# Attention and token-mixing MLP in one kernel: a ramp by halves of 256 tokens, a halved last pass, quarter-row MLP pieces, and a planner without its table of rules

## The chip, the cores and the metric

The kernel runs on one core of one Trainium2 chip. The metric is the device time of one launch in microseconds (us). Before the change it is 755.73 us, the median of 3 runs (755.54 to 755.74).

## What is computed

For 2048 tokens of width 640, with 32 heads of width 20:

```python
xn = layernorm(x)
q, k, v = xn @ wqkv                        # 32 heads of 20
s = softmax(q @ k.T * 20 ** -0.5) @ v @ wo # s: [2048, 640]
u = gelu(w1.T @ layernorm(xn) + b1)        # over tokens: 2048 -> 1536
y = w2.T @ u + b2                          # 1536 -> 2048
out = x + s * silu(y)
```

The attention has 32 heads x 2048 queries x 2048 keys of scores, and each score needs an exponential. The MLP mixes along the tokens, not along the features.

## The kernel before, in words

**Units and passes.** Heads go in 8 groups G of four. A pass is one group and 512 queries, so there are 32 passes (`passes`, L852). In a pass the keys come in 16 chunks of 128. A unit is one head, one chunk and 512 queries: a score tile of 128 keys x 512 queries that fills one PSUM bank. A pass has 64 units and the program 2048. A head's 20 rows are padded to 32, so the four heads of a group lie in the four row groups of the PE array. One visit of PE to the scores (`emit_st`, L1206) runs up to four units side by side, one in each row group.

**Two ways to take an exponential.** ACT takes most units: one Exp over two or three banks (`emit_exp`, L1235) from PSUM to the ring `pt_sb` (20 slots). DVE takes the others. It turns a score into a bf16 bit pattern by an add and a maximum (`emit_op1`, L1246), and for each four units of a chunk it makes three shifted copies (`emit_top`, L1268). The weighted sum of four such patterns stands for the exponential. Only the chunks in `RC` may go to DVE. The weighted sums with v (`emit_pv`, L1284) add up in the bank `AB`; at the end of a pass `ep_steps` (L1400 to L1421) transposes that bank, divides by the row sums and stores.

**Banks.** Two ACT groups of three banks (0 to 2, 3 to 5), the bank `AB` of the sums, and one bank `JB` for everything else. The third bank of an ACT group can be lent to a DVE unit (`LEND`), and then the Exp covers two banks.

**The rest of the work** is cut in jobs that take bank `JB` one after the other: projections for the next groups (`dqk_steps`), v (`v_steps`), the two MLP matmuls (`mlp_steps`, 16 or 12 steps of K=128 for 512 columns, each step four 32-column matmuls side by side at L644) with their activations (`act_steps`, L829 to L845), and the output projection (`op_mms`, L929) with its product (L944) and the residual (L954).

**Order of work.** All of it is fixed on the host. A planner keeps a reckoned clock for each engine, with a cost for each instruction (`mm`, `dv`, `ac`) and a hand-over time between engines (`Prog.lat`). At each turn it takes, on the engine that is free first, the candidate of the best priority (`pe_cands`, `eng_cands`). A switch of PE between scores, sums and full matmuls counts some 105 ns (`pe_cost`). `act_deadline` says by when the next scores are due, and `SLACK` by how much other work may overrun that. `PLAN` is a table of rules: for each 16 units it picks one of the values in `OPTS` for 14 settings (`tune`).

**Ramp.** x comes in six DMAs of one to four 128-token blocks. `ln_steps` takes the statistics of a block on DVE (L531, L533, L538, L542), the inverse root on POOL (L545) and applies it on DVE (L549). The first 512 tokens are transposed on PE (L598), the others by DMA (L586). `qk_steps` (L629) makes q and k of group 0, `v_steps` (L737) v. `wp_step` (L720) copies the first 80 columns of wq and wk into padded form on ACT. The ramp ends for the planner when the last v (`v0_14`) and the last q (`qk0_0_3`) are made; only then do DVE units begin.

**Tail.** The last pass ends with its transposes by halves (L1392 to L1396). The last 512 tokens are then finished: matmuls for what is known already (L929) before, the last head group's part (L934) after, products with the gate (L1607, L1623), the residual (L1609, L1625) and four stores (L1616).

The softmax here doesn't subtract the row's maximum and nothing guards it: scores larger than these inputs give would overflow.

## Time and profile before

| what | value |
|---|---|
| median of 3 runs | 755.73 us |
| span of the profiled execution, first to last instruction | 753.7 us |
| left between the span and the median | 2.0 us (755.73 - 753.7) |
| ACT busy | 729.9 us (97%), 695 instructions |
| DVE busy | 721.0 us (96%), 1320 instructions |
| PE busy | 717.6 us (95%), 10302 matmuls |
| POOL busy | 15.6 us (2%) |
| DMA | 42.54 MB, mean 56 GB/s |

The page gives no time of its own for the profiled execution besides its span. So the 2.0 us between the span and the median are what lies around it, and I take them as fixed. "Busy" is the time in which an engine has at least one instruction running. For PE it also holds waiting in its pipeline, so three figures near 96% don't say which engine sets the end. The chain of waits and a table by stages tell that.

### The profile page before, as it was taken

How to read it: one execution, taken by the hardware profiler on the slowest of the kernel's cores; microseconds unless marked ns; L12 is line 12 of the kernel's file. 1: busy time of each engine (PE TensorE's matmuls, PEld its weight loads, DVE VectorE, ACT ScalarE, POOL GpSimd, SP SyncE). 2: the span in 40 equal slices, each digit the busy share in tenths (PEclk: the TensorE clock that was granted, in tenths of full speed). 3: DMA queues.
4: the chain of work that ended last, by engine and by line, in shares of the span. 5: the costliest groups of instructions: out<-in, count | busy, mean ns of one | idle time of the engine just before them, and what ended most of it. 6: DMA issues, size and time to landing. Idle time of an engine off the chain costs nothing.

```text
span 753.7 us, 23158 instructions
## 1 busy us (share of the span) xinstructions
PE 717.6 (95%) x10302; PEld 240.7 (32%) x10302; DVE 721.0 (96%) x1320; ACT 729.9 (97%) x695; POOL 15.6 (2%) x22
## 2 busy tenths in 40 slices
PE   9999999999999999999999999999999988998997
PEld 7432223222323232323223323233333232222222
DVE  8869999999999999999999999999999999999997
ACT  4999999999999999999999999999999999999993
POOL 4200000000000000000000000000000000000001
PEclk9999999999999999999999999999999999999999
DMA  9584111110313031121014022223124340011011
GB/s 245 109 167 57 38 26 38 20 36 7 86 14 77 13 68 38 35 61 21 7 37 111 26 49 52 47 54 102 44 57 82 76 150 11 6 47 48 13 47 36
DMA packets 117143, 42.54 MB, mean 56 GB/s; under 512 B 75300, under 2 KB 115876, under 8 KB 116996
## 3 DMA queue, kind: packets, MB, share of 16 engines
q1 hardware_dynamic: 117044, 41.07, 23.9%
q8 instruction: 80, 1.31, 0.7%
q14 instruction: 19, 0.16, 0.1%
HBM read 26.37 MB, written 10.22 MB: 49 GB/s over the span
## 4 chain that ended last, share of the span: by engine, by line
ACT 85%; PE 12%; DVE 2%; DMA 1%; issue 0%; POOL 0%
ACT pt_sb L1235 83%; PE ps_all L1284 4%; PE ps_all L644 4%; PE ps_all L1206 4%; ACT zt_sb L840 1%; ACT zt_sb L835 1%; PE ps_all L929 1%; DMA xnT_sb<-regC 1%; DVE bst_sb L531 0%; DVE bst_sb L533 0%; DMA regA<-in_A_x_dram 0%; DVE regC L549 0%; DVE regC L1607 0%; PE ps_all L683 0%; DVE xnT_sb L611 0%
## 5 line engine op out<-in xcount | busy, mean ns | idle before, releaser
L1235 ACT ACTIVATE pt_sb<-ps_all 128x1024 bf16<-128x1024 f32 (+1 forms) x672 | 710.5, 1226 | 2.4 <-PE ps_all L1206 1.9
L1246 DVE TENSOR_SCALAR dt_sb<-ps_all 128x512 uint16<-128x512 f32 x496 | 328.2, 684 | 10.1 <-PE ps_all L1206 8.3
L1206 PE MATMUL ps_all<-qk_sb 32*128 32x512 bf16 x2048 | 266.7, 384 | 27.7 <-ACT pt_sb L1235 24.8
L1268 DVE TENSOR_SCALAR dt_sb<-dt_sb 128x2048 uint16<-128x2048 uint16 x372 | 241.9, 687 | 1.4
L1206 PEld LDWEIGHTS ps_all<-qk_sb 32*128 32x128 bf16 x2048 | 67.0, 91 | 283.8 <-ACT pt_sb L1235 231.8
L1284 PE MATMUL ps_all<-dt_sb,vs_sb 128*21 128x512 bf16 x1488 | 124.6, 382 | 0.8 <-DVE dt_sb L1268 0.7
L1284 PE MATMUL ps_all<-pt_sb,v_sb 128*21 128x512 bf16 x1552 | 124.2, 382 | 0.9 <-DVE tr_sb L1400 0.6
L644 PE MATMUL ps_all<-regB,regA 128*32 128x128 bf16 (+1 forms) x1536 | 68.2, 301 | 0.7 <-DVE regB L845 0.3
L644 PE MATMUL ps_all<-regC,regA 128*32 128x512 bf16 (+1 forms) x1536 | 68.4, 301 | 0.0
L1284 PE MATMUL ps_all<-dt_sb,v_sb 128*21 128x512 bf16 x496 | 49.0, 384 | 0.3 <-DVE tr_sb L1400 0.2
L644 PE MATMUL ps_all<-xnT_sb,wqk_sb 128*32 128x512 bf16 x640 | 48.2, 382 | 0.3 <-DVE zt_sb L814 0.2
L1284 PEld LDWEIGHTS ps_all<-dt_sb,vs_sb 128*21 128x21 bf16 x1488 | 31.5, 91 | 41.3 <-issue 21.9
L1284 PEld LDWEIGHTS ps_all<-pt_sb,v_sb 128*21 128x21 bf16 x1552 | 28.7, 90 | 47.7 <-issue 38.0
L644 PEld LDWEIGHTS ps_all<-regB,regA 128*32 128x32 bf16 x1536 | 27.2, 96 | 27.0 <-issue 13.1
L644 PEld LDWEIGHTS ps_all<-regC,regA 128*32 128x32 bf16 x1536 | 27.3, 96 | 25.6 <-issue 13.4
L929 PE MATMUL ps_all<-wv_sb,xnT_sb 128*128 128x128 bf16 (+3 forms) x160 | 29.5, 302 | 0.1
L644 PE MATMUL ps_all<-wv_sb,xnT_sb 128*32 128x480 bf16 x320 | 23.0, 369 | 0.0
L1400 DVE STREAM_TRANSPOSE tr_sb<-ps_all 128x512 f32<-128x512 f32 x31 | 22.1, 711 | 0.9 <-PE ps_all L1284 0.7
L644 PEld LDWEIGHTS ps_all<-xnT_sb,wqk_sb 128*32 128x32 bf16 x640 | 13.7, 95 | 18.2 <-issue 7.7
L1284 PEld LDWEIGHTS ps_all<-dt_sb,v_sb 128*21 128x21 bf16 x496 | 12.6, 90 | 21.3 <-issue 14.7
L814 DVE TENSOR_SCALAR zt_sb<-ps_all,b2h_sb 128x512 bf16<-128x512 f32 (+1 forms) x32 | 17.2, 544 | 0.0
L1044 DVE CAST v_sb<-ps_all 128x480 bf16<-128x480 f32 (+1 forms) x22 | 13.4, 610 | 3.3 <-PE ps_all L737 3.1
(82 smaller groups left out, 307.0 us busy)
## 6 DMA issues: line engine op xcount, KB each, us to landing
regA<-in_B_w_dram SPq DMA_DIRECT2D x6, 1024.0 KB
regA<-in_B_w_dram SPq DMA_DIRECT2D x8, 768.0 KB
qk_sb<-qk_scratch_dram SPq DMA_DIRECT2D x56, 80.0 KB
qk_scratch_dram<-qs_sb SPq DMA_DIRECT2D x32, 128.0 KB
regA<-in_A_x_dram SPq DMA_DIRECT2D x6, 640.0 KB
ok_scratch_dram<-on_sb SPq DMA_DIRECT2D x96, 20.0 KB
out_dram<-regC SPq DMA_DIRECT2D x3, 640.0 KB
wqk_sb<-in_A_wqkv_dram SPq DMA_DIRECT2D x2, 480.0 KB
```

Source lines behind the costliest of these rows:

```text
L644: fns.append(lambda e, c=c, e_=e_: e.matmul(oc(c, e_), lhsT[:, c:e_], rhs, start=start, stop=stop, tile_position=(0, c)))
L814: steps.append(("dve", lambda e, z=z, i=i, jj=jj: e.tensor_scalar(z[:, c0:c0 + n], ps(bk, n, i * n), 0.5, bias[:, jj:jj + 1], ALU.mult, AL ...
L835: steps.append(("act", lambda e: e.activation(tt_, tt_, AF.Tanh, scale=1.5957691216), [stt], [stt], f"th{j}", ac(n)))
L840: steps.append(("act", lambda e: e.activation(tt_, z, AF.Tanh), sz, [stt], f"th2_{j}", ac(n)))
L929: steps.append(("pe", lambda e, c=c, k=k: e.matmul(ap, oT_sb[0:k, c, b * 128:(b + 1) * 128], wo_ap[0:k, c, c0:c0 + n], start=(opens and c ...
L1044: return lambda e: e.tensor_copy(dst, src)
L1206: pr.pe(lambda e, outp=outp, lhsT=lhsT, rhs=rhs, g=g: e.matmul(outp, lhsT, rhs, start=True, stop=True, tile_position=(32 * g, 0)), reads=[ ...
L1235: tk = pr.act(lambda e: e.activation(outp, inp, AF.Exp, scale=math.log(2.0) / 128.0), reads=[bank_slot[b] for b in banks[:n]], writes=[S_( ...
L1246: tk = pr.dve(lambda e: e.tensor_scalar(w, src, WOFF, 0.0, ALU.add, ALU.max), reads=[bank_slot[bk]], writes=[S_(f"dt{d['tl'][0]}_{g}")], n ...
L1268: tk = pr.dve(lambda e: e.tensor_scalar(dst, src, dk, None, ALU.add), reads=[S_(f"dt{b0}_{g}") for g in range(4)], writes=[S_(f"dt{b}_{g}" ...
L1284: pr.pe(lambda e: e.matmul(outp, lhsT, rhs, start=(k == 0), stop=last, tile_position=(0, 32 * g)), reads=reads, writes=[bank_slot[AB]], na ...
L1400: steps.append(("dve", lambda e: e.transpose(tr_sb[:, :], ps(AB)), [bank_slot[AB]], [S_("tr")], f"epT{q}", 632.0))
```

## The change

- **Hand-overs.** The planner reckons 39 ns more from PE to ACT, 12 ns more from PE to DVE and 40 ns between dependent instructions on DVE.
- **Rules.** `PLAN` is empty. Fixed values stand in its place: SLACK 0 instead of 120, D_GUARD 8 instead of 16, LATE 1 instead of 2, EVP 36 instead of 24, ACTP 22 instead of 30; with four or more free slots in `pt_sb` jobs go ahead of sums (`JOBF`). `RC` becomes 0, 3, 6, 9, 12.
- **Ramp.** The first 512 tokens go in two halves of 256: transposes, evictions, q and k for each half. Only 80 columns of wq and wk are loaded early; the other 176 come after x. A first small ACT instruction brings the table load ahead. The LayerNorm goes in pairs of blocks throughout, and the first blocks' application no longer waits for the statistics of blocks 2 and 3. In pass 0 the first four units hold two chunks of 256 queries each. The ramp ends when the last k and the second q are made. ACT group 0's banks are kept free from the start.
- **Last pass.** It is cut into two passes of 256 queries, each of 8 x 4 units of two chunks. Token blocks 12 and 13 become ordinary output jobs after the first half, and only blocks 14 and 15 remain for the tail.
- **Quarter-row pieces.** Where a score visit leaves a row group free, `row_piece` puts one quarter (32 rows) of an MLP step into it. A step whose four quarters went that way is not run on its own. No two such pieces run at once, and a PE wait on the piece before is added where it is needed.
- **Output columns.** The last 128 output columns of two blocks share one bank and one product (`op2_steps`).

```diff
-        return 0.0 if src == eng else self.LAT[eng] + (40.0 if eng == "act" and src == "pe" else 45.0 if eng == "dve" and src == "pe" else 0.0)
+        return (40.0 if eng == "dve" else 0.0) if src == eng else self.LAT[eng] + (79.0 if eng == "act" and src == "pe" else 57.0 if eng == "dve" and src == "pe" else 0.0)
...
+        if after is not None and t.klg[self.cidx_of["pe"]] >= after.cidx > self.known["pe"][self.cidx_of["pe"]]:
+            t.waits["pe"] = after
+            after.need_inc = True
+            self.known["pe"][self.cidx_of["pe"]] = after.cidx
...
-    RC = (2, 5, 8, 11, 14)
+    RC = (0, 3, 6, 9, 12)
...
-    D_GUARD = 16
-    MLP_A, MLP_B = 2.6, 24.0
+    D_GUARD = 8
+    MLP_A, MLP_B = 2.6, 23.0
     QK_LEAD = 6.0
-    SLACK, MINJ = 120.0, 640.0
+    SLACK, MINJ = 0.0, 640.0
     ROOM = 3
+    ROWM, ROWP, ROWN = 5, 2, 400
...
+    RAMPEND = ('qk0_1_3', 'qk0_0_1')
+    RLEND = 0
+    DRDY = 'xn15'
...
-    LATE = 2.0
+    LATE = 1.0
...
+    JOBF = 4
...
-    PLAN = (
...
+    PLAN = ()
...
+        dma_w(0, 80, wqk_sb[:, :, 0, 0:80], S_("wq0"))
+        dma_w(640, 80, wqk_sb[:, :, 1, 0:80], S_("wk0"))
...
-        dma_w(0, 256, wqk_sb[:, :, 0, 0:256], S_("wq"))
-        dma_w(640, 256, wqk_sb[:, :, 1, 0:256], S_("wk"))
...
+        dma_w(80, 176, wqk_sb[:, :, 0, 80:256], S_("wq"))
+        dma_w(720, 176, wqk_sb[:, :, 1, 80:256], S_("wk"))
...
+        pr.act(lambda e: e.activation(cst_sb[:, 2:3], cst_sb[:, 0:1], AF.Copy), reads=[S_("mhalf")], writes=[S_("tl")],
+               name="tl", cost=1400.0)
...
+                if lhsT.shape[1] == 128 and not start and not stop:
+                    row = lambda g: (lambda e: e.matmul(oc(0, 128), lhsT[32 * g:32 * g + 32, :], rhs[32 * g:32 * g + 32, :],
+                                                        start=False, stop=False, tile_position=(32 * g, 0)))
...
-        passes += [(L6, 0), (L6, 1), (L7, 0), (L7, 1), (L6, 2), (L7, 2), (L6, 3), (L7, 3)]
...
+        passes += [(L6, 0), (L6, 1), (L7, 0), (L7, 1), (L6, 2), (L7, 2), (L6, 3), (L7, 3), (L7, 3)]
...
+        HALF = {NP - 2: 0, NP - 1: 1}
+        HP = ((0, 1), (3, 4), (6, 7), (9, 10), (12, 13), (14, 15), (2, 5), (8, 11))
+        units, dunits = [], []
+        for q, (G, p) in enumerate(passes):
+            if q in HALF:
+                a = 256 * HALF[q]
+                units.append([[(c0, p * 512 + a, 256, 0, a), (c1, p * 512 + a, 256, 256, a)] for c0, c1 in HP])
+                dunits.append([(6, (0, 1)), (7, (2, 3))])
+            else:
+                units.append([[(c, p * 512, 512, 0, 0)] for c in range(NB)])
+                dunits.append([(c, (r,)) for r, c in enumerate(RC)])
+                if q == 0:
+                    units[0][:4] = [[(c, a, 256, 0, a), (c + 1, a, 256, 256, a)] for c in (0, 2) for a in (0, 256)]
+                    dunits[0] = [x for x in dunits[0] if x[0] >= 4]
...
+        def op2_steps(bs):
+            def make(bk):
+                n = len(bs)
+                steps = []
+                for i, b in enumerate(bs):
+                    steps += op_mms(b, ps(bk, 128, 128 * i), 512, 128, bank_slot[bk])
+                g = regC[:, bs[0]:bs[0] + n, 512:640]
+                pp = ps(bk, 128 * n).rearrange("p (i n) -> p i n", i=n)
+                steps.append(("dve", lambda e: e.tensor_tensor(g, pp, g, ALU.mult),
+                              [bank_slot[bk]] + [S_(f"g{b}") for b in bs], [S_(f"r{b}_1") for b in bs],
+                              f"prod{bs[0]}", dp(128 * n)))
...
-        freebanks = [3, 4, 5, 0, 1, 2, JB]
-        retired = set()
+        freebanks = [3, 4, 5, JB]
+        retired = set(self.ACT_GROUPS[0])
...
-        LN = ((0, 2), (2, 2), (4, 2), (6, 2), (8, 4), (12, 4))
+        LN = ((0, 2), (2, 2), (4, 2), (6, 2), (8, 2), (10, 2), (12, 2), (14, 2))
         for i, (b0, nb) in enumerate(LN):
-            rq = () if i < 4 else (f"xn{LN[i - 1][0] + LN[i - 1][1] - 1}",)
+            rq = () if i < 4 else (f"lnv{LN[i - 1][0]}",)
...
+                for h in (0, 1):
+                    hp = "" if h else "a"
+                    for dcs in ((0, 1), (2, 3), (4,)):
+                        add_bank_job(f"xT{h}_{dcs[0]}", xT_steps(h, dcs), (f"xn{2 * h}", f"xn{2 * h + 1}"), 18.0 + h)
+                    xh = tuple(f"xT0{hp}_{d}" for d in (0, 2, 4))
+                    add_bank_job(f"q0_0{hp}", qk_steps(0, 0, 256 * h, 256, hp), (f"xT0{hp}_0", "wp0_0"), 17.0 if h == 0 else 22.4)
+                    add_bank_job(f"k0_0{hp}", qk_steps(1, 0, 256 * h, 256, hp), (f"xT0{hp}_0", "wp0_1"), 17.1 if h == 0 else 22.5)
...
+                for ch, col, m, off, _ in units[q][c]:
+                    lhsT = qk_sb[32 * g:32 * g + 32, slot, 1, ch * 128:(ch + 1) * 128]
+                    rhs = qk_sb[32 * g:32 * g + 32, slot, 0, col:col + m]
+                    outp = ps(bk, m, off)
+                    pr.pe(lambda e, outp=outp, lhsT=lhsT, rhs=rhs, g=g: e.matmul(outp, lhsT, rhs, start=True, stop=True,
+                                                                                tile_position=(32 * g, 0)),
+                          reads=qslots(slot, p, col, m, g) + [S_(kslot(slot, ch, g))] + ([S_(f"qkp_{g}")] if slot else []),
+                          writes=[bank_slot[bk]], name=f"st{q}_{c}_{g}", cost=cost / np_, w=53.0 / np_)
...
+        NL = 2
+        LB = [NB - NL + i for i in range(NL)]
...
-            if late:
+            if late or (self.JOBF and room >= self.JOBF):
...
+        def row_piece(used):
+            free = [g for g in range(4) if g not in used]
+            if not free or ramp[0] or len(used) != len(set(used)):
+                return
+            prev = self.lastrow
+            if prev is not None and prev.fin + 60.0 > pr.T["pe"]:
+                return
+            best = None
+            for j in active:
+                if j.bk is None or j.i >= len(j.steps) or j.steps[j.i][0] not in ("pe", "row"):
+                    continue
+                for i, gs in j.rows.items():
+                    for g in free:
+                        if g in gs:
+                            best = (j, i, g)
+                            break
+                    if best:
+                        break
+                if best:
+                    break
+                if sum(1 for x in j.rows.values() if x) >= self.ROWP:
+                    continue
+                e = j.i
+                n = 0
+                while e < len(j.steps) and j.steps[e][0] in ("pe", "row"):
+                    n += j.steps[e][0] == "pe"
+                    e += 1
+                if n < self.ROWM or j.steps[j.i][0] != "pe" or j.steps[j.i][5] < 180.0 or j.i == 0 or j.steps[j.i - 1][0] not in ("pe", "row"):
...
+            j, i, g = best
+            x = j.rowstep[i]
+            j.rows[i].discard(g)
+            self.lastrow = pr.pe(x[7](g), reads=x[2], writes=x[3], name=x[4] + "r", cost=4.0, w=53.0, after=prev)
+            stats["rows"] = stats.get("rows", 0) + 1
+            settle(j)
...
-            if ramp[0] and "v0_14" in done and "qk0_0_3" in done:
+            if ramp[0] and all(x in done for x in self.RAMPEND):
                 ramp[0] = False
-            if not dveready[0] and "qk0_1_3" in done:
+            if not dveready[0] and self.DRDY in done:
```

## Prediction

> **What bounds the kernel now.** I read the page's head and chain first: they say which engine's work ends last.
>
> ```profile
> span 753.7 us, 23158 instructions
> ...
> ACT 85%; PE 12%; DVE 2%; DMA 1%; issue 0%; POOL 0%
> ```
>
> The chain runs through ACT. Next the busy time by stages (columns: stretch, length, then PE, PE loads, DVE, ACT, POOL with counts, clock, DMA).
>
> ```profile
> 0.00:10.00 10.00, 8.81 (x81) 8.54 (x82) 7.15 (x25) 2.26 (x4) 6.30 (x13) 1.00 0.79 242
> 10.00:20.00 10.00, 9.62 (x99) 6.49 (x100) 8.72 (x34) 7.32 (x9) 1.92 (x3) 1.00 1.01 234
> 20.00:30.00 10.00, 8.73 (x91) 3.75 (x91) 8.79 (x29) 10.00 (x9) 1.48 (x2) 1.00 0.48 68
> 30.00:40.00 10.00, 9.22 (x104) 4.13 (x101) 7.98 (x31) 10.00 (x8) 3.04 (x2) 1.00 0.80 196
> 40.00:50.00 10.00, 8.72 (x70) 3.10 (x74) 4.92 (x12) 9.18 (x8) 0.00 (x0) 1.00 0.73 179
> ...
> 60.00:740.00 680.00, 652.77 (x9673) 208.19 (x9665) 666.42 (x1162) 679.34 (x651) 0.63 (x1) 1.00 0.20 47
> 740.00:754.00 14.00, 9.92 (x78) 3.60 (x77) 8.06 (x19) 1.76 (x2) 2.26 (x2) 1.00 0.13 47
> ```
>
> From 60 to 740 us ACT idles 0.66 us of 680 and DVE 13.6 us. The middle is bound by the work on ACT, with DVE close behind. What is idle lies at the ends: ACT 10.4 us in the first 20, 0.8 at 40 to 50, 12.2 in the last 14; DVE 8.3 us between 20 and 50. The third view, the groups by form, prices a unit.
>
> ```profile
> L1235 ACT ACTIVATE pt_sb<-ps_all 128x1024 bf16<-128x1024 f32 x464 | 450.7, 1089 | 0.5 <-PE ps_all L1206 0.2
> L1246 DVE TENSOR_SCALAR dt_sb<-ps_all 128x512 uint16<-128x512 f32 x496 | 328.2, 684 | 10.1 <-PE ps_all L1206 8.3
> L1235 ACT ACTIVATE pt_sb<-ps_all 128x1536 bf16<-128x1536 f32 x208 | 301.2, 1530 | 1.9 <-PE ps_all L1206 1.7
> ...
> L1268 DVE TENSOR_SCALAR dt_sb<-dt_sb 128x2048 uint16<-128x2048 uint16 x372 | 241.9, 687 | 1.4
> ```
>
> ACT does 464 x 2 + 208 x 3 = 1552 units. Its two forms overlap, and together they are busy 710.5 us on the page: 0.458 us a unit. DVE does 496 units at 328.2 / 496 + 241.9 / 496 = 1.149 us. Together they do 2.18 + 0.87 = 3.05 units a us, and the planner can move units between them. So 1 us of idle that is filled on ACT shortens the program by 2.18 / 3.05 = 0.71 us, on DVE by 0.29 us. I use these weights below.
>
> **The Trainium skill.** "TensorEngine Tiling (Array Packing)", Key Properties, says that changing the tiling mode drains the PE, and Gotcha 1 that row tiles can't write the same bank at once. So a quarter-row piece is free of a switch beside scores, and two of them must not overlap; no row of before shows such a piece. "ScalarE: Activation LUTs", What ACT_TABLE_LOAD costs, gives 1283 ns, and the trace has 1283. "DMA: Bandwidth & Descriptors", Specifications, asks for 512 B for full rate; the 80-column loads have 160 B rows, and the trace shows no such load of weights. "VectorE: DVE Perf Modes", the TRN2 errata, says that each instruction pays a fixed latency. The trace agrees: the eviction at L611 took 676 ns for 1024 elements and 418 for 512.
>
> **The ramp.** The ACT timeline of before (start, length):
>
> ```profile
> 7.62 1.28 ACT L720 ACT_TABLE_LOAD   x1 [7.62 <-DMA wqk_sb<-in_A_wqkv_dram]
> ...
> 15.62 4.13 ACT L1235 ACTIVATE pt_sb<-ps_all 128x1536 bf16<-128x1536 f32 x3 [0.48 <-PE ps_all L1206]
> 19.79 0.38 ACT L1043 ACTIVATE qk_sb<-ps_all 128x256 bf16<-128x256 f32 x1
> 20.07 12.19 ACT L1235 ACTIVATE pt_sb<-ps_all 128x1536 bf16<-128x1536 f32 x9
> ```
>
> Exps start at 15.62 and run without a break from 20.07; by then 9 units are done. After the change: the inverse root of blocks 0 and 1 ends at 6.41, as before, since POOL's memset of v holds it back to 5.58. Two applications 0.80, ten PE transposes 0.72, evictions of half the width 0.6 (DVE 0.42 measured at 512; ACT between 0.5 and 0.7 from its 1.02 at 1024), ten 256-column matmuls 1.4 (five took 0.72), evictions 0.4, scores 0.4 and hand-overs 0.2: first exp at 10.9. The weights must be there by 8.5. Before they came at 7.6; 160 B rows can cost more, but 320 KB of x and 2 x 176 columns now come behind them, so I take 6.5, and the table load is done by then. The second half follows some 2 us later. The first 512 x 512 block gives 16 units, 7.3 us of ACT. So about 15 units are done by 20 instead of 9: 6 x 0.458 = 2.75 us of ACT, x 0.71 = **2.0 us**. The bound below is 0.5: if the next k, whose DMA transpose lands at 18.55 before, comes late, ACT stands still there. The late 176-column loads run in the SP queue ahead of these transposes: 0.45 MB at the 361 GB/s that the trace has from 12 to 14 us is 1.3 us.
>
> DVE units begin at 49.8 before, after the last q. They now begin after the last k (38.4 before) and second q, and the pairwise LayerNorm brings k forward. Of 8.3 us idle I take 5 as filled: x 0.29 = **1.4 us** (0 to 2.4). Of ACT's hole of 0.8 us at 44, half: **0.3**. What is added lies on SP, POOL and DVE: two more inverse roots (0.7 each on an idle POOL), some 0.1 us instructions on DVE. The sum is 3.7 us.
>
> **The tail.** Last pieces before:
>
> ```profile
> 740.76 1.45 ACT L1235 ACTIVATE pt_sb<-ps_all 128x1536 bf16<-128x1536 f32 x1 [0.46 <-PE ps_all L1206]
> ...
> 743.31 0.45 DVE L1392 STREAM_TRANSPOSE tr_sb<-ps_all 128x256 f32<-128x256 f32 x1 [1.88 <-PE ps_all L1284]
> ...
> 745.25 0.45 DVE L1396 STREAM_TRANSPOSE stage_sb<-on_sb 128x256 bf16<-128x256 bf16 x1
> ...
> 746.09 1.33 DVE L1607 TENSOR_TENSOR regC<-ps_all,regC 128x512 bf16<-128x512 f32 x2 [0.40 <-PE ps_all L934]
> ...
> 750.83 0.42 DVE L1609 TENSOR_TENSOR regC<-regC,regA 128x512 bf16<-128x512 bf16 x1
> ```
>
> From the start of the transposes to the end of DVE it takes 751.25 - 743.31 = 7.94 us for four blocks. After: one half's transpose, reciprocal, product, transpose, 0.45 + 0.20 + 0.28 + 0.45 = 1.4; a matmul and hand-over 0.5; then two products 0.6 each, the joined one 0.4, two additions 0.3 + 0.4 (the third is on POOL): 2.3. Sum 4.2, so 3.7 us less, at full weight, since both engines idle there. What moves into the second half's exps: on DVE two products, a joined one, two residuals, 2 x 0.68 + 0.42 + 2 x 0.48 = 2.7, and a half's epilogue 1.4, 4.1 us in all; 1.88 us of it finds DVE waiting as shown, the other 2.2 x 0.29 = 0.6. If that wait is gone, 1.2. PE gets some 3 us of output matmuls and the store of 12 and 13 goes on SP; both have room. Scores and sums of 256 columns double PE's instructions in the last pass, but five matmuls of that width in 0.72 us stand 0.11 apart, half the 0.216 of a full one, so I price that at nothing (up to 1 us of PE, hidden under ACT). The second half's sums wait for the first half's transpose (0.45); the ring holds 20 units meanwhile. The tail gives **3.0 us** (2.0 to 3.7).
>
> **The middle.** Joined columns: 12 x 0.275 on DVE become 6 x 0.42: 0.8 x 0.29 = **0.2**. Quarter-row pieces: at most two open in a job at a time, 28 MLP jobs, 1 to 2 steps of 0.216 each: 6 to 12 us off PE, against some 10 ns a piece (a visit of four takes 0.40 against 0.39), 1 to 2 us. PE is not the bound: ACT's scores wait 0.66 us. It helps where DVE waits for scores, 8.3 us at L1246: 0 to 2.4 us, and I take 0.6. A piece can also hold JB until enough visits have passed; priced from the same row, a unit's score late by a visit (0.9 us) in 28 jobs is 25 x 0.29 = 7 us at the very worst, more likely below 1. The added PE wait has only scores and sums behind it and is placed where the piece before is done: nothing. The rules: not visible in the trace. Longer hand-overs should bring the order nearer to the chip, the empty table takes away choices window by window. ACT at 99.9% can hardly gain; I take a loss of 0.6 us (0 to 14, below). The middle gives 0.2.
>
> **Sum:** 3.7 + 3.0 + 0.2 = 6.9 us. The profiled execution goes from 753.7 to 746.8 in span; with the 2.0 us around it, 748.8, against the median of 755.7.
>
> **The rivals.** (1) *The order opens up.* Without rules chosen for each window PE serves ACT late. Every visit that comes late stops ACT; with 30 ns in the mean (my assumption, under a third of a switch's 105 ns in the planner) 672 exps x 30 ns = 20 us, x 0.71 = 14, and 748.8 + 14 = 762.8. From 10 us of ACT idle in the middle on, it eats the whole gain. For it: PE has 27 us left in 680, and with SLACK 0 work is refused whenever it seems not to fit, so jobs pile up toward the end. Against it: longer hand-overs ask for scores earlier, and the pieces take load off PE. (2) *The early start is not used:* k comes no earlier, ACT starves at 19, the ring fills before v is there, and only the tail's lower bound of 2.0 remains, less 0.5 for the rules: 755.7 - 1.5 = 754.2. For it: the landing at 18.55 and the loads put ahead of it; against it: blocks 4 and 5 need only their own statistics. (3) *The middle gains:* the scores that DVE waits for come in time, its 13.6 us halve (6.8 x 0.29 = 2.0), the rules cost nothing (0.6) and the ramp's idle on DVE is used fully (1.0): 748.8 - 3.6 = 745.2. For it: PE's relief and an earlier k; against it: ACT has only 0.66 us to give.
>
> **How the numbers follow.** The forecast has 0.54, with its own range of 746 to 753; (3) has 0.12, (2) 0.10, (1) 0.24. About 0.2% (1.5 us) can be told from no change: 754.2 and 757.2 bound "the same". Faster gets 0.54 + 0.12 + half of (2) and a little less for the edge: 0.69; same 0.08; slower 0.23. The range of 743 to 758.5 takes in (3), (2) and the first part of (1), and leaves out about 0.2, nearly all of it above.
>
> **What would show it.** Right: first exp near 11 and 14 to 16 units by 20 us; DVE units from about 37; from transposes to the last DVE instruction 4 to 5 us; ACT idle under 3 us from 60 to the last half. Wrong: ACT idle above 10 us in the middle with PE named as the releaser, fewer than 480 units on DVE, or a hole in ACT near 19 us.

## The result, and the profile after

The changed kernel takes 756.58 us, the median of 20 runs (756.08 to 758.77), against 755.82 us for 20 runs of the kernel before beside them: a ratio of 1.0008, 95% interval 1.0002 to 1.0014. That is practically no change, where the forecast was 6.9 us less. The profiled execution has a span of 755.5 us, 1.8 more than the 753.7 of before. It took 757.3 us, 0.7 more than the median, so 1.8 us between the two spans stand for 0.8 us between the medians.

The head and the chain of waits, from the page of the kernel after:

```profile
span 755.5 us, 23583 instructions
...
ACT 84%; PE 11%; DVE 3%; DMA 1%; SPq 0%; issue 0%
```

The chain still runs through ACT. The busy time by stages of the kernel after (columns as in the prediction: stretch, length, PE, PE loads, DVE, ACT, POOL, clock, DMA):

```profile
0.00:10.00 10.00, 8.03 (x78) 7.59 (x79) 6.41 (x23) 3.16 (x5) 6.31 (x13) 1.00 0.76 219
10.00:20.00 10.00, 8.83 (x120) 6.20 (x118) 10.00 (x37) 8.02 (x9) 2.09 (x3) 1.00 1.08 233
20.00:30.00 10.00, 8.28 (x101) 3.86 (x101) 8.77 (x36) 7.70 (x7) 2.11 (x3) 1.00 0.72 123
30.00:40.00 10.00, 8.38 (x80) 3.32 (x75) 8.04 (x27) 9.64 (x9) 3.04 (x2) 1.00 0.81 207
40.00:50.00 10.00, 8.98 (x96) 3.83 (x94) 10.00 (x24) 9.82 (x11) 0.00 (x0) 1.00 0.56 138
...
60.00:740.00 680.00, 647.33 (x9804) 209.54 (x9808) 656.10 (x1143) 677.38 (x657) 0.63 (x1) 1.00 0.20 47
740.00:756.00 16.00, 10.49 (x140) 5.46 (x135) 11.39 (x23) 4.80 (x5) 1.33 (x1) 0.98 0.24 83
```

Subtract each busy time from its length and set the rest against the same row of before.

| idle, us | before | after | forecast of the step |
|---|---|---|---|
| ACT, 0 to 20 | 10.4 | 8.8 | 2.75 less |
| ACT, 20 to 60 | 0.8 | 2.8 | 0.4 less |
| DVE, 20 to 50 | 8.3 | 3.2 | 5 less |
| ACT, 60 to 740 | 0.66 | 2.62 | about the same |
| DVE, 60 to 740 | 13.6 | 23.9 | a little less |
| last exp to last DVE instruction | 9.04 | 8.40 | some 3.7 less |

So the start of the ramp came as forecast, ACT gave it back between 20 and 60 us, and the middle lost. The groups by form of the kernel after show the division of the units and DVE's waits:

```profile
L1308 ACT ACTIVATE pt_sb<-ps_all 128x1024 bf16<-128x1024 f32 x495 | 484.2, 1106 | 2.1 <-PE ps_all L1376 1.4
L1319 DVE TENSOR_SCALAR dt_sb<-ps_all 128x512 uint16<-128x512 f32 x496 | 327.7, 679 | 18.8 <-PE ps_all L1279 9.7 <-PE ps_all L656 6.9
L1308 ACT ACTIVATE pt_sb<-ps_all 128x1536 bf16<-128x1536 f32 x187 | 278.7, 1524 | 4.0 <-PE ps_all L1279 3.8
```

DVE still does 496 units, so the division of units is that of before. At 60 us DVE was ahead: it had finished 16 units instead of 8, and ACT 92 instead of 94. Over the whole program DVE's lead came back as waits: its idle time before its score operation rose from 10.1 us (L1246 before) to 18.8 (L1319). The new idle time is no even spread: between 60 us and the last exp five single waits of DVE, of 0.9 to 1.8 us, make 7.1 us, where before has no wait of DVE over 1.05. During the three longest (they end at 101.0, 234.7 and 570.8 us) PE ran projection or MLP matmuls (L648) for 1.05 to 1.26 us, twice ahead of the scores that DVE waited for, once as the work that it waited for. One wait of ACT, 1.42 us before 593.75, makes half of ACT's 2.62.

**The ramp.** The ACT timeline of the kernel after (start, length):

```profile
11.93 1.45 ACT L1308 ACTIVATE pt_sb<-ps_all 128x1536 bf16<-128x1536 f32 x1
14.69 2.79 ACT L1308 ACTIVATE pt_sb<-ps_all 128x1536 bf16<-128x1536 f32 x2 [1.31 <-PE ps_all L1279]
...
22.06 6.82 ACT L1308 ACTIVATE pt_sb<-ps_all 128x1536 bf16<-128x1536 f32 x5 [0.50 <-PE ps_all L1279]
30.23 5.48 ACT L1308 ACTIVATE pt_sb<-ps_all 128x1536 bf16<-128x1536 f32 x4 [1.35 <-PE ps_all L1279]
```

The first exp starts at 11.93 instead of 15.62, but ACT now has holes before 14.69, 22.06 and 30.23, where before ran without a break from 20.07. Before 14.69 the last input made was the q and k of the second half of the tokens, which DVE had evicted at 13.94. The chain of waits of the kernel after, in order of time, names what the two later holes wait for:

```profile
3.64 4.79 DMA regA<-in_A_x_dram
8.46 0.49 DVE bst_sb L530
...
16.80 3.57 DMA xnT_sb<-regC
20.42 0.72 PE ps_all L633 x5
...
28.02 0.51 DVE v_sb L1114
28.57 0.72 PE ps_all L633 x5
```

Blocks 4 and 5 of x land at 8.43, behind the weights; DVE waits 0.77 us for them with the first half's work queued behind. The k of these blocks starts on PE (L633) at 20.42, after the DMA transpose. That transpose lands at 16.80 + 3.57 = 20.37, where the prediction read 18.55 for before: this k did not come forward with the pairwise LayerNorm, it came 1.8 us later. The next k starts at 28.57, when a v job has freed the one bank for jobs.

**The tail.** DVE's timeline of the kernel after:

```profile
746.45 0.45 DVE L1492 STREAM_TRANSPOSE tr_sb<-ps_all 128x256 f32<-128x256 f32 x1 [1.38 <-PE ps_all L1376]
...
747.05 0.64 DVE L980 TENSOR_TENSOR regC<-ps_all,regC 128x512 bf16<-128x512 f32 x1
...
748.70 0.42 DVE L994 TENSOR_TENSOR regC<-ps_all,regC 128x256 bf16<-128x256 f32 x1 [0.30 <-PE ps_all L970]
...
749.64 1.84 DVE L1006 TENSOR_TENSOR regC<-regC,regA 128x640 bf16<-128x640 bf16 x2
...
752.78 0.42 DVE L1716 TENSOR_TENSOR regC<-regC,regA 128x512 bf16<-128x512 bf16 x1
```

From the transposes to the end it takes 753.20 - 746.45 = 6.75 us, against 7.94 before and 4.2 forecast. L980, L994 and L1006 are the output jobs of blocks 12 and 13, which the forecast had inside the second half's exps: 0.64 + 0.42 + 1.84 = 2.9 us of them lie in the tail. The first half's epilogue ends at 739.5, the last exp at 744.80, and these jobs pass through the one bank JB in turn.

### The profile page after: what moved, and what is told of

Same layout as the page of the kernel before. It is cut to its first block, busy times and chain, and to the rows that moved or that the text cites. A ratio compares the mean times of both kernels' runs of the same rounds, so it can differ in the third digit from the quotient of the medians.

```text
span 755.5 us, 23583 instructions
## 1 busy us (share of the span) xinstructions
PE 709.7 (94%) x10508; PEld 242.5 (32%) x10520; DVE 720.5 (95%) x1321; ACT 730.5 (97%) x708; POOL 15.5 (2%) x23
## 3 DMA queue, kind: packets, MB, share of 16 engines
q1 hardware_dynamic: 119636, 41.15, 23.6%
## 4 chain that ended last, share of the span: by engine, by line
ACT 84%; PE 11%; DVE 3%; DMA 1%; SPq 0%; issue 0%
ACT pt_sb L1308 82%; PE ps_all L648 4%; PE ps_all L1279 4%; PE ps_all L1376 3%; ACT zt_sb L849 1%; ACT zt_sb L844 1%; DMA regA<-in_A_x_dram 1%; DVE regC L568 1%; DMA xnT_sb<-regC 0%; PE ps_all L965 0%; PE ps_all L633 0%; DVE bst_sb L530 0%; DVE bst_sb L532 0%; DVE dt_sb L1319 0%; DVE v_sb L1114 0%
## 5 line engine op out<-in xcount | busy, mean ns | idle before, releaser
L1308 ACT ACTIVATE pt_sb<-ps_all 128x1024 bf16<-128x1024 f32 (+2 forms) x683 | 711.7, 1220 | 6.1 <-PE ps_all L1279 3.8
L1319 DVE TENSOR_SCALAR dt_sb<-ps_all 128x512 uint16<-128x512 f32 x496 | 327.7, 679 | 18.8 <-PE ps_all L1279 9.7
L1279 PE MATMUL ps_all<-qk_sb 32*128 32x512 bf16 (+1 forms) x2128 | 268.6, 376 | 32.5 <-ACT pt_sb L1308 28.9
L1279 PEld LDWEIGHTS ps_all<-qk_sb 32*128 32x128 bf16 x2128 | 68.3, 91 | 289.5 <-ACT pt_sb L1308 243.8
L1376 PE MATMUL ps_all<-pt_sb,v_sb 128*21 128x512 bf16 (+1 forms) x1616 | 127.0, 374 | 2.3 <-DVE v_sb L1114 1.0
L1376 PE MATMUL ps_all<-dt_sb,vs_sb 128*21 128x512 bf16 (+1 forms) x1536 | 124.1, 375 | 0.1
L648 PE MATMUL ps_all<-regB,regA 128*32 128x128 bf16 (+1 forms) x1492 | 63.6, 299 | 0.0
L648 PE MATMUL ps_all<-regC,regA 128*32 128x128 bf16 (+1 forms) x1448 | 62.5, 296 | 0.1
L1376 PE MATMUL ps_all<-dt_sb,v_sb 128*21 128x512 bf16 (+1 forms) x512 | 49.0, 378 | 0.3 <-issue 0.3
L1376 PEld LDWEIGHTS ps_all<-pt_sb,v_sb 128*21 128x21 bf16 x1616 | 32.9, 91 | 50.9 <-issue 32.5
L648 PE MATMUL ps_all<-xnT_sb,wqk_sb 128*32 128x512 bf16 x640 | 45.6, 382 | 0.2 <-DVE qs_sb L1117 0.2
L648 PEld LDWEIGHTS ps_all<-regB,regA 128*32 128x32 bf16 x1492 | 26.9, 96 | 25.2 <-issue 12.9
L648 PEld LDWEIGHTS ps_all<-regC,regA 128*32 128x32 bf16 x1448 | 26.2, 96 | 24.9 <-issue 14.0
L656 PE MATMUL ps_all<-regC,regA 32*128 32x512 bf16 x88 | 33.9, 385 | 0.0
L965 PE MATMUL ps_all<-wv_sb,xnT_sb 128*128 128x128 bf16 (+1 forms) x150 | 25.4, 296 | 1.9 <-issue 1.1
L1500 DVE STREAM_TRANSPOSE tr_sb<-ps_all 128x512 f32<-128x512 f32 x31 | 21.9, 706 | 0.0
L648 PE MATMUL ps_all<-wv_sb,xnT_sb 128*32 128x480 bf16 x320 | 21.1, 369 | 0.0
L648 PEld LDWEIGHTS ps_all<-xnT_sb,wqk_sb 128*32 128x32 bf16 x640 | 13.2, 95 | 18.4 <-issue 8.1
```

What stands on the lines that cost most here:

```text
L648: fns.append(lambda e, c=c, e_=e_: e.matmul(oc(c, e_), lhsT[:, c:e_], rhs, start=start, stop=stop, tile_position=(0, c)))
L656: row = lambda g: (lambda e: e.matmul(oc(0, 128), lhsT[32 * g:32 * g + 32, :], rhs[32 * g:32 * g + 32, :], start=False, stop=False, tile_p ...
L965: steps.append(("pe", lambda e, c=c: e.matmul(ap, oT_sb[:, c, b * 128:(b + 1) * 128], wo_ap[:, c, c0:c0 + n], start=(opens and c == 0), st ...
L1279: pr.pe(lambda e, outp=outp, lhsT=lhsT, rhs=rhs, g=g: e.matmul(outp, lhsT, rhs, start=True, stop=True, tile_position=(32 * g, 0)), reads=q ...
L1308: tk = pr.act(lambda e: e.activation(outp, inp, AF.Exp, scale=math.log(2.0) / 128.0), reads=[bank_slot[b] for b in banks[:n]], writes=[S_( ...
L1319: tk = pr.dve(lambda e: e.tensor_scalar(w, src, WOFF, 0.0, ALU.add, ALU.max), reads=[bank_slot[bk]], writes=[S_(f"dt{d['tl'][0]}_{g}")], n ...
```

## The experiments

**Theories.** (A) *The order.* Both kernels are orders fitted to one exact reckoning of the planner; emptying the table and changing costs throws the old fit away, and what the parts gain is spent on that. (B) *A part costs:* pieces, loads ahead of x, joined output or a setting of the planner loses in its own place what ramp and tail win. (C) *The parts gain nothing*, and the rules cost nothing either. The letters in the expectations quoted below belong to each expectation alone.

The table has all runs, e1 to e18, which are described below it: time, ratio to the kernel before as it ran beside each (755.57 to 756.19 us) with its 95% interval, then from the profile the end of the last exp, what follows until DVE's last instruction, and the idle time of ACT and DVE from 60 us to the last exp. All in us.

| run | time | ratio | last exp | after it | ACT idle | DVE idle |
|---|---|---|---|---|---|---|
| before | 755.82 | 1 | 742.2 | 9.0 | 1.1 | 14.4 |
| after | 756.58 | 1.0008 [1.0002, 1.0014] | 744.8 | 8.4 | 2.6 | 23.9 |
| e1 | 763.88 | 1.0103 [1.0089, 1.0117] | 751.6 | 8.1 | 3.5 | 31.5 |
| e4 | 770.72 | 1.0192 [1.0179, 1.0206] | 758.5 | 8.3 | 4.0 | 43.9 |
| e9 | 765.46 | 1.0128 [1.0112, 1.0145] | 749.8 | 12.1 | 3.9 | 30.0 |
| e13 | 768.42 | 1.0173 [1.0159, 1.0187] | 758.4 | 8.2 | 5.9 | 41.8 |
| e2 | 793.81 | 1.0501 [1.0487, 1.0516] | 742.6 | 46.3 | 3.6 | 25.5 |
| e5 | 771.48 | 1.0197 [1.0173, 1.0220] | 753.9 | 9.4 | 4.3 | 45.1 |
| e6 | 774.00 | 1.0235 [1.0221, 1.0249] | 754.5 | 14.9 | 10.4 | 32.0 |
| e7 | 779.20 | 1.0304 [1.0290, 1.0318] | 746.3 | 28.7 | 6.2 | 27.5 |
| e3 | 761.18 | 1.0068 [1.0054, 1.0082] | 746.8 | 10.3 | 5.8 | 25.0 |
| e8 | 759.41 | 1.0050 [1.0037, 1.0062] | 742.6 | 12.6 | 2.6 | 23.8 |
| e10 | 764.14 | 1.0116 [1.0101, 1.0131] | 749.2 | 10.5 | 2.7 | 32.8 |
| e11 | 767.26 | 1.0156 [1.0141, 1.0171] | 745.6 | 17.0 | 1.2 | 28.3 |
| e12 | 762.22 | 1.0086 [1.0071, 1.0101] | 748.9 | 8.4 | 7.3 | 26.5 |
| e17 | 760.60 | 1.0059 [1.0047, 1.0071] | 747.6 | 7.9 | 5.8 | 26.3 |
| e18 | 784.13 | 1.0371 [1.0358, 1.0385] | 742.9 | 37.0 | 3.1 | 28.2 |
| e14 | 756.71 | 1.0008 [1.0002, 1.0015] | 745.1 | 8.4 | 4.3 | 25.4 |
| e15 | 757.26 | 1.0019 [1.0012, 1.0026] | 744.2 | 8.4 | 2.7 | 23.6 |
| e16 | 756.31 | 1.0006 [0.9999, 1.0012] | 744.2 | 7.5 | 2.8 | 23.8 |

### The table of rules and the settings

**e1**, the kernel before with its table empty:

```diff
-    PLAN = ("00000000000010", "00000000000000", ...)
+    PLAN = ()
```

> The kernel before with its table of rules emptied and nothing else changed. Theory A (the table kept the middle full, and its loss ate what the ramp and the tail gave): 3 to 8 us slower than before, with ACT idle of over 2 us and DVE idle of over 20 us between 60 and 740 us. Theory B (the table was worth little; ramp and tail gave nothing of themselves): within 1.5 us of before.

It took 763.88 us, some 8 more. The stages of e1:

```profile
60.00:740.00 680.00, 649.65 (x9604) 206.71 (x9596) 654.41 (x1142) 676.80 (x653) 0.63 (x1) 1.00 0.20 46
```

DVE's idle time in this stretch is 680 - 654.41 = 25.6 us instead of 13.6, ACT's 3.2 instead of 0.66. These are about the values of the kernel after, 23.9 and 2.62: a loss in the middle of the same size, from this one edit. DVE did 488 units here instead of 496.

**e4**, e1 with the new hand-overs:

```diff
-        return 0.0 if src == eng else self.LAT[eng] + (40.0 ... else 45.0 ...)
+        return (40.0 if eng == "dve" else 0.0) if src == eng else self.LAT[eng] + (79.0 ... else 57.0 ...)
```

> The kernel before with its table emptied and the longer hand-overs, all else as before. Theory D: at least 1 us faster than the same without them (e1). Theory C: at least 1 us slower than e1, with fewer units on DVE. Either way it is slower than before by 2 to 8 us if the table was worth that.

770.72 us, 6.8 more than e1, with 480 units on DVE instead of 488. In this order the longer hand-overs brought no gain.

**e9**, e4 with the fixed values of the change, so that the planner's settings are nearly those of after while the work is that of before (`V1A` and `V1B`, which the change sets too, are included, `VPRIO` and `RC` are not):

```diff
-    D_GUARD = 16
-    MLP_A, MLP_B = 2.6, 24.0
+    D_GUARD = 8
+    MLP_A, MLP_B = 2.6, 23.0
...
-    SLACK, MINJ = 120.0, 640.0
+    SLACK, MINJ = 0.0, 640.0
...
-    LATE = 2.0
+    LATE = 1.0
...
-    ACTP = 30.0
+    ACTP = 22.0
...
-    TOPP, EVP = 38.0, 24.0
+    TOPP, EVP = 38.0, 36.0
...
-    V1A, V1B = 0.8, 4.0
+    V1A, V1B = 1.2, 3.0
...
-            if late:
+            if late or room >= 4:
```

> The kernel before with the planner's side of the change alone: table emptied, longer hand-overs, SLACK 0, D_GUARD 8, LATE 1, EVP 36, ACTP 22, MLP_B 23, V1A and V1B 1.2 and 3.0, jobs ahead of sums at four free slots; ramp, last pass, pieces, columns, RC and VPRIO as before. Theory A (the planner's side costs what the rest of the change gives): 4 to 8 us slower than before, DVE idle in the middle over 20 us. Theory P (the prediction's working: 0.6 us): within 1.5 us of before, and then the ramp must have cost what halves and pieces gave.

765.46 us: in this order the fixed values did not stand in for the table.

**e5**, the kernel after with the table of before:

```diff
-    PLAN = ()
+    PLAN = ("00000000000010", "00000000000000", ...)
```

> The kernel after with the table of before put back (it sets SLACK and 13 others again for each 16 units, around the old defaults). Theory A1 (choices window by window are worth something in any order of work): 3 to 8 us faster than after, 749 to 754. Theory A2 (the table is fitted to the one order that it was made for, and its value, 7.8 us on the kernel before, is gone once the work is ordered otherwise): no faster than after, or up to 15 us slower.

771.48 us, 14.9 more than the kernel after: here the table made for one order was worse than none for another.

**e2**, **e6** and **e7**, the kernel after with one setting back at its old value each:

```diff
-        return (40.0 if eng == "dve" else 0.0) if src == eng else self.LAT[eng] + (79.0 ... else 57.0 ...)
+        return 0.0 if src == eng else self.LAT[eng] + (40.0 ... else 45.0 ...)
```

> The kernel after with the hand-over times of before (95 ns from PE to ACT, 100 from PE to DVE, none on the same engine). Theory C (the longer reckoned hand-overs make the planner believe DVE busier than it is, so it hands it fewer units): 1 to 4 us faster than after, more than 496 units on DVE or DVE idle under 15 us in the middle. Theory D (they bring the order nearer to the chip): slower than after by 1 to 5 us, with more of ACT's idle ending at PE's scores.

```diff
-    SLACK, MINJ = 0.0, 640.0
+    SLACK, MINJ = 120.0, 640.0
```

> The kernel after with SLACK 120 instead of 0. If SLACK 0 is what keeps ACT fed without the table: 3 to 10 us slower, with more ACT idle ending at PE. If with the longer hand-overs it only holds back the jobs: 1 to 4 us faster.

```diff
-    JOBF = 4
+    JOBF = 0
```

> The kernel after without the rule that jobs go ahead of sums when four slots of the exp ring are free. If that rule is what keeps MLP and output jobs in time: over 5 us slower, with output jobs left after the last exp. If not: within 2 us of after.

They took 793.81, 774.00 and 779.20 us. In e2 and e7 the last exp ends within 2.3 us of the kernel after; what they lose lies behind it, 46.3 and 28.7 us instead of 8.4, with output jobs that were not done in time. DVE did 504 units in e2, more than 496 as that expectation's first theory had it, and the time rose all the same. These two settings changed when jobs got the bank, more than how ACT was fed. e6 loses on both sides, 10.4 us of ACT idle and 14.9 us after the last exp. Each of these seven runs is one newly planned order; how far a new order alone can move the time is measured below.

### One part at a time, planned anew

**e3**, the kernel after without pieces:

```diff
-            if not free or ramp[0] or len(used) != len(set(used)):
+            if True or not free or ramp[0] or len(used) != len(set(used)):
```

> The kernel after without the quarter-row pieces. If the 33 steps that they save on PE (7 us) matter for the middle: 1 to 3 us slower than after. If PE is not what holds ACT or DVE: within 1 us of after. If the pieces themselves hold back DVE's scores (6.9 us of DVE idle end at them in the trace): 1 to 2 us faster, and DVE idle in the middle falls toward 17 us.

**e8**, the kernel after with a whole last pass and the tail of before:

```diff
-        passes += [..., (L6, 3), (L7, 3), (L7, 3)]
+        passes += [..., (L6, 3), (L7, 3)]
...
-        HALF = {NP - 2: 0, NP - 1: 1}
+        HALF = {}
```

> The kernel after with the last pass whole and the tail of before (four blocks, two of its additions on POOL), all else as after. The prediction's own working (the halved pass gives 3.0 us): 3 us slower than after. Theory T (output jobs of blocks 12 and 13 spill past the last exp, so the halves give under 1 us): within 1 us of after; from the start of the last transposes to the last DVE instruction 7.5 to 8.5 us instead of 6.75.

**e10**, the load of blocks 4 and 5 ahead of the weights' first columns:

```diff
+        dma_x(4, 2)
...
-        dma_x(4, 2)
```

> The kernel after with the DMA of blocks 4 and 5 of x issued ahead of the two 80-column weight loads. If that landing (8.43 us in the trace of after, with DVE waiting 0.77 us for it and the evictions of the first half queued behind) delays the ramp: DVE doesn't wait at its statistics of block 4, and the first exp comes 0.3 to 1.0 us earlier. The weights then come later, and if the ACT copies of them (6.03 and 7.59) set the first exp instead, it stays at 11.9 or later. In total time at most 1 us either way, plus what a changed order of the middle brings.

They took 761.18, 759.41 and 764.14 us. Read by themselves, they say that the pieces are worth 4.6 us, the halves 2.8, near the 3.0 forecast, and that the order of the loads costs 7.6 where at most 1 was forecast. The next group shows that none of these values can be trusted.

### A nanosecond in the reckoning

Three kernels with the same work as after or before and one reckoned cost a little higher. **e11** is after and **e13** before (with its table) with

```diff
-            return max(n / 2.4 + 3.0, 60.0)
+            return max(n / 2.4 + 4.0, 60.0)
```

in `mm`, the reckoned cost of the full matmuls (projections, MLP, output); **e12** is after with DVE's score operation reckoned 2 ns longer:

```diff
-                   writes=[S_(f"dt{d['tl'][0]}_{g}")], name=f"dw{d['q']}_{d['c']}_{g}", cost=601.0)
+                   writes=[S_(f"dt{d['tl'][0]}_{g}")], name=f"dw{d['q']}_{d['c']}_{g}", cost=603.0)
```

> The kernel after with one reckoned cost changed: 4 ns instead of 3 of fixed cost for each full matmul in the planner. Nothing that a kernel does is changed by it, only when the planner thinks that things are done, so it measures how much of a difference is mere reordering. If the planner's order is robust: within 0.5 us of after. If it amplifies: 2 us or more either way, and differences of that size between single edits (4.6 us for the pieces, 2.8 for the halves) are then not theirs alone.

> The kernel before, its table kept, with 4 ns instead of 3 of reckoned fixed cost for a full matmul. If the table is fitted to one exact order: 5 to 12 us slower than before, as the kernel after was (10.7). If the table's choices make the order robust: within 2 us of before, and then the change gave away that robustness.

> The kernel after with another reckoned cost changed: 603 ns instead of 601 for a DVE score tile. As for the run with 1 ns on the matmuls: within 0.5 us of after if the order is robust, 2 us or more either way if the planner amplifies small changes.

After became 10.7 and 5.6 us slower, before 12.6. The stages of e12, and then of e13:

```profile
60.00:740.00 680.00, 643.07 (x9685) 205.80 (x9688) 653.54 (x1134) 672.69 (x650) 1.10 (x1) 1.00 0.20 47
```

```profile
60.00:740.00 680.00, 645.04 (x9495) 205.16 (x9504) 642.73 (x1114) 674.84 (x645) 1.18 (x1) 0.99 0.20 46
```

In e12 ACT's ramp is no worse than that of after (idle 8.9 and 2.2 us in 0 to 20 and 20 to 60, against 8.8 and 2.8), yet ACT idles 7.31 us from 60 to 740 instead of 2.62. In e13 DVE idles 37.3 us instead of 13.6, with the whole table still there. The work is the same; which of several nearly equal candidates comes first differs, and each such turn moves all later ones. In e13 this also moved 16 units from DVE to ACT (480 on DVE instead of 496); in e12 DVE still did 496.

**e17** and **e18** repeat the comparisons of e8 and e3 under e12's 603 ns; their edits are those of e8 and e3, each with e12's:

```diff
-        HALF = {NP - 2: 0, NP - 1: 1}
+        HALF = {}
...
-            if not free or ramp[0] or len(used) != len(set(used)):
+            if True or not free or ramp[0] or len(used) != len(set(used)):
```

> The changed kernel with the last pass whole and the tail of before, as in the earlier run with a whole last pass, but planned with 603 instead of 601 ns reckoned for DVE's score operation. The work is that of the earlier run; only the order differs. It is to be read against the kernel with 603 ns and a halved last pass (762.2 us). If the halves are worth a fixed 2 to 4 us at the end of the program, this kernel takes 764 to 767. If the 2.8 us seen between the two kernels at 601 ns were mostly the planner's scatter, it lands anywhere from 756 to 772, and the sign may turn. In its trace the time from the first to the last operation of the tail (transposes to last DVE instruction) should again be about 7.2 us.

> The changed kernel without quarter-row pieces (every MLP step is run whole), planned with 603 instead of 601 ns reckoned for DVE's score operation. To be read against the kernel with 603 ns and pieces (762.2 us). If the pieces themselves are worth the 4.6 us that their removal cost at 601 ns, it takes 766 to 768. If that was the planner's scatter, since 33 steps are only 7 us on an engine that has about 30 us of idle time, it lands within 756 to 772 with no fixed sign, and PE busy rises by some 7 us whatever the time.

e17 took 760.60 us against 762.22 for e12: the sign turned, and the halves now cost 1.6 us instead of bringing 2.8. Its tail, transposes to end, is 7.18 us as in e8 (7.16); e12's is 6.91, after's 6.75. So from the transposes on, the halves bring only 0.3 to 0.4 us. Most of what e8 lost lay elsewhere: 5.4 us from the last exp to the transposes, against 1.65 in the kernel after, though its last exp ended 2.2 us earlier. e18 took 784.13, and the "worth" of the pieces went from 4.6 to 21.9 us. ACT's timeline of e18 at the end, and then DVE's:

```profile
717.80 25.09 ACT L1308 ACTIVATE pt_sb<-ps_all 128x1024 bf16<-128x1024 f32 x23
```

```profile
742.97 0.69 DVE L980 TENSOR_TENSOR regC<-ps_all,regC 128x512 bf16<-128x512 f32 x1 [0.70 <-PE ps_all L965]
...
766.99 0.42 DVE L994 TENSOR_TENSOR regC<-ps_all,regC 128x256 bf16<-128x256 f32 x1 [0.94 <-PE ps_all L970]
```

The last exp ends at 742.89, earlier than in the kernel after. Then 25 us of output jobs (L980, L994, L1006) follow one after the other through the bank, each with PE and DVE waiting for the other. That is no price of 33 MLP steps run whole, some 7 us of PE; it is an order in which the output jobs were left to the end. Neither 4.6 nor 21.9 us is the price of the pieces.

### One edit, all the rest of the order kept

**e14**: the order as planned for after; only the load of blocks 4 and 5 is issued ahead of the weights' when the program is written out.

```diff
-            self.schedule()
+            self.schedule(); sp = pr.tasks["sp"]; ...; sp.insert(i, sp.pop(k))
```

> The kernel after with its order of work kept on every engine; only the issue of blocks 4 and 5 of x moves ahead of the two 80-column weight loads on SP. If their late landing costs the ramp what the trace shows (DVE waits 0.77 us at 8.46): first exp up to 0.8 us earlier, or later if the weights then come last; in total time 0 to 0.7 us faster, as ACT is bound by k again at 20 us. 0.5 us slower at most.

756.71 us, the same as after. The first exp came at 11.21, 0.72 us earlier, and DVE no longer waits for x; but ACT stood still all the same for 1.27 us before 13.93 and 1.35 before 28.71. The lead was 1.5 us by then (28.71 against 30.23), and ACT still had it at 592.26 (593.75 in after). It went in one pause of PE, 1.66 us before 596.8, for which the trace names no cause. This execution took 757.6 us, 0.9 above the median of e14, so whether the others have the pause is not known; the median shows no gain. e10, the same move planned anew, was 7.6 us slower than after; with the order kept, the move itself cost nothing.

**e15**: pieces of 8 columns instead of 512, in the same order.

```diff
-                    row = lambda g: (lambda e: e.matmul(oc(0, 128), lhsT[...], rhs[32 * g:32 * g + 32, :],
+                    row = lambda g: (lambda e: e.matmul(oc(0, 128)[:, 0:8], lhsT[...], rhs[32 * g:32 * g + 32, 0:8],
```

> The kernel after with its order kept; the 132 quarter-row pieces run 8 of their 512 columns, so 33 MLP steps are left out but for these columns. If the pieces ride free beside the scores: within 0.5 us of after. If they hold up the scores or DVE (6.9 us of DVE idle end at them): 1 us or more faster.

757.26 us, 0.7 more than after where at most 0.5 was forecast, and not faster. The groups of e15 by form:

```profile
L1319 DVE TENSOR_SCALAR dt_sb<-ps_all 128x512 uint16<-128x512 f32 x496 | 328.6, 681 | 18.6 <-PE ps_all L1279 16.5
...
L1279 PE MATMUL ps_all<-qk_sb 32*128 32x512 bf16 x1968 | 258.6, 384 | 31.7 <-ACT pt_sb L1308 28.2
```

These means are over all score matmuls, and only 132 of the visits carry a piece. Taken apart in the trace of after, a visit of three score matmuls lasts 393 ns in the mean without a piece (515 visits) and 398 with one (132); back to back, the next matmul starts 321 ns after the visit's start without a piece and 325 with one. So a full piece costs some 4 ns, 0.5 us of PE in all. DVE's wait is 18.6 us in e15 against 18.8. The 6.9 us that the kernel after puts down to L656 go to L1279 here: the piece was only the matmul of the visit that ended last. The pieces ride almost free, and nothing is won by making them short.

**e16**: the one addition of the tail that POOL does goes to DVE.

```diff
-            steps.append(("pool" if i < 1 else "dve", lambda e: e.tensor_tensor(g0, g0, regA[:, b, 0:512], ALU.add),
+            steps.append(("pool" if i < 0 else "dve", lambda e: e.tensor_tensor(g0, g0, regA[:, b, 0:512], ALU.add),
```

> The kernel after with the last POOL addition of the tail done on DVE; the order changes only in the last six DVE instructions. In the trace of after the two residual additions beside POOL take 1.84 us together instead of 0.88. If POOL slows DVE there: 0.4 to 0.6 us faster (0.96 regained, 0.34 to 0.42 added on DVE). If not: 0.4 slower.

756.31 us. DVE's timeline of e16:

```profile
749.02 0.48 DVE L1006 TENSOR_TENSOR regC<-regC,regA 128x640 bf16<-128x640 bf16 x1
749.42 0.42 DVE L1716 TENSOR_TENSOR regC<-regC,regA 128x512 bf16<-128x512 bf16 x1
749.75 0.48 DVE L1006 TENSOR_TENSOR regC<-regC,regA 128x640 bf16<-128x640 bf16 x1
```

The two additions take 0.48 us each instead of 1.84 together, and transposes to end 5.88 us instead of 6.75. In the medians it shows as 0.3 us, less than the 0.4 to 0.6 forecast, with an interval that overlaps that of after: inside the scatter of the runs.

## Why the prediction was wrong

**The weights hold here.** With 0.71 us for 1 us of ACT idle and 0.29 for DVE, the measured idle times give: ramp +0.4 x 0.71 - 6.0 x 0.29 (DVE, 20 to 60: 9.4 before, 3.4 after) = -1.4; middle, from 60 us to the last exp, +1.5 x 0.71 + 9.5 x 0.29 = +3.8; after the last exp -0.6. The sum is +1.8, and the span rose by 1.8. The forecast had -3.7, -0.2 and -3.0. So the errors are 2.3, 4.0 and 2.4 us. Over the whole span of e12, with 496 units on DVE, the weights give +5.7 where +6.3 was measured; of e13, with 480, +11.4 where +15.2 was measured.

**The step that failed most** is the one on the planner's rules in the middle: "Longer hand-overs should bring the order nearer to the chip, the empty table takes away choices window by window. ACT at 99.9% can hardly gain; I take a loss of 0.6 us (0 to 14, below)." The size was too small, 0.6 us where the middle lost 3.8, and the reason was wrong too. I treated 99.9% of ACT and 13.6 us of DVE idle as a property of the work, to which the edits add and subtract. It belongs to one order. The kernel before loses 8 us with its table emptied (e1), and 12.6 us with the table kept and 1 ns added to a reckoned cost (e13). So the 8 us cannot be called the worth of the rules; they are within what a new order can cost. The first rival had the place right, the order of the middle. Its mechanism, PE late for ACT with 10 us or more of ACT idle, did not happen (2.62); by the weights, 2.8 of the 3.8 us are DVE's. The views show PE late, but for DVE: the few long waits named above, which stand at the same places of the order in e14, e15 and e16.

**The ramp's start** was right in its steps: first exp at 11.93 (10.9 forecast; 12.05 and 11.66 in e15 and e16, which have this order), 15 units by 20.5 us (forecast: about 15 by 20), first DVE unit at 37.9 (37), DVE's idle time 5.1 us less at 20 to 50 (5). What failed was to take 2.0 us for it rather than the lower bound of 0.5, which named the case: "if the next k ... comes late, ACT stands still there". It did: that k came not forward but 1.8 us later, so the step "the pairwise LayerNorm brings k forward" failed for this first k. In e15 and e16, which have the same ramp, ACT idles 2.2 and 2.3 us from 20 to 60, so some 0.6 of the 2.8 us belong to this one execution. That a still earlier start (e14) brings nothing in the median stays unexplained, since its trace kept the lead to 592 us. The second rival was half right on this: ACT's lead was lost, DVE's earlier start remained.

**The tail** failed in one term: the products and additions of blocks 12 and 13 were all placed inside the second half's exps (priced at 0.6 us), and 2.9 us of them came after, 0.9 of it because POOL held up an addition. The views of before could have warned of it: there is one bank for jobs, and half a pass lasts only 32 / 3.05 = 10.5 us, in which the first half's epilogue has to come first.

**The middle's small terms.** The pieces' 10 ns were priced near enough (some 4 ns measured). That the doubled count of matmuls in the last pass costs nothing was not tried alone. The 0.6 us from the pieces' relief of PE cannot be seen: PE's busy time from 60 to 740 fell by 5.4 us (652.77 to 647.33), and the time did not follow. The joined columns, the new `RC` and the LayerNorm by pairs were not tried alone either. Two rivals count a term twice: 762.8 holds the 0.6 us for the rules besides the 14, and 745.2 the 0.6 for the pieces besides the halved waits that it comes from. This changes neither reading.

**What is shown and what is not.** Shown: the kernel before without its table is 8 us slower; three changes of the reckoning by 1 or 2 ns, all that were made, cost 5.6 to 12.6 us; ACT's lead in the ramp is lost while it waits for k; the tail holds 2.9 us of moved work. Not settled: what the parts are worth together, and why the middle of this one order waits more than that of before. Kernels with the work of before and no table took 763.9 to 770.7 us (three), those with the work of after and its settings, in orders it was not fitted to, 762.2 to 767.3 (e10, e11, e12). That fits a gain of a few us from the parts which the lost table takes back, theory A, but the scatter is as large as the gain, so it stays argued, and that both kernels are fitted orders is inferred from these slower ones. The same holds for the runs with a setting changed or put back (e2, e4 to e7, e9): e18 shows that even a small edit, planned anew, can cost 21.9 us. B falls for the pieces (e15), the loads (e14) and POOL's addition (e16), each within 0.7 us with the order kept; for the settings and the joined columns it stays open. C falls with e1 in so far as the rules did not cost nothing. No run beat the kernel before.

## What to carry to other kernels

Where the order is made by a greedy planner, first change a reckoned cost by a nanosecond and leave the work alone: the scatter this gives (here 5.6 to 12.6 us) is the least that a replanned part must gain before its time means anything. Price a part with the order kept and the one thing changed, and count a fitted table as part of the kernel's speed, which any other edit discards. An earlier start of the bounding engine is worth only what its next inputs allow, so follow the second and third input too, not only the first.

## What the runs showed of the hardware

- **POOL's addition blocks DVE's.** Beside POOL's addition (1.33 us from 749.81) one of the two additions at L1006 took 1440 ns; the median of that line is 480. The Trainium skill, "SBUF — State Buffer", section "SBUF: two separate sides", says that the shared port pair is an exclusive lock and that "the other fully blocks". The trace agrees: the addition that starts at 750.0 ends 0.3 us after POOL does. In e16, without POOL's addition, both take 0.48.
- **A row-tile matmul in a free row group costs the visit next to nothing:** three score matmuls took 393 ns in the mean alone and 398 beside a full piece. This agrees with the skill's "TensorEngine Tiling (Array Packing)", Key Properties, where tiles work independently.
- **Loads ahead in the queue held up x:** the two loads of 80 columns, 100 KB each, landed at 6.0 and 7.6 us, and the 320 KB of x issued after them at 8.43. With x issued first (e14) DVE did not wait for it. No run changed the width of the rows alone, so whether the narrow rows are to blame is not shown.
